# A fused linear-attention and gated feed-forward kernel: the second product from fp32r to fp16 pairs

## The chip, the cores and the metric

The kernel runs on one core of one Trainium2 chip. The metric is the device time of one execution in microseconds (us); less is better. Engines are named as in the profile: PE is TensorE's matmul, PEld its weight load, DVE is VectorE, ACT is ScalarE, POOL is GpSimd and SP is SyncE, which here issues the transfers (DMAs).

## The reference

Two stages follow each other. The first is a linear attention with the delta rule, token by token, for 4 sequences of 768 tokens and 8 heads of width 48. The second is a gated feed-forward product without an activation function.

```python
for t in range(S):
    kt, vt, bt = (k_n[:, :, t], v[:, :, t], beta[:, :, t, None])
    y[:, :, t] = np.einsum('bhd,bhde->bhe', q[:, :, t], state)
    v_old = np.einsum('bhde,bhd->bhe', state, kt)
    state = state + bt[:, :, :, None] * np.einsum('bhd,bhe->bhde', kt, vt - v_old)
...
a = x @ w_a
b = x @ w_b
return (a * b @ w_out).astype(np.float32)
```

`k_n` is k over its norm, x holds the 3072 tokens' y with 384 columns, w_a and w_b are 384 x 1536, w_out is 1536 x 384, all in fp32. So there are a *first product* (x with w_a and with w_b), a *gate* (a times b), and a *second product* (the gate's result with w_out).

## The kernel before

**Attention.** The 768 steps are cut into 24 chunks (`NCH`) of 32 tokens; one chunk holds 4 sequences x 32 tokens = 128 rows. Six groups of four chunks are prepared together: `prep` computes the norms of k and the 32 x 32 inner products, `solve` inverts the triangular systems on DVE (31 steps of two operations, or two halves of 15 for the first two groups), and `steps` runs the recurrence chunk by chunk: the state `S_ps` is copied to `sh`, multiplied with k and q (`yp`), the difference `f` is formed on DVE, multiplied by the inverse (`up`, copied to `u`), and `u` updates `S_ps` and completes `yp`. Then y is scaled and moved to `y32` (an ACT copy of one half, a DVE operation that adds the other), transposed in 32 x 32 blocks on DVE (`yT`), and split into a high and a low fp16 part (`xv`, in tiles `xb` or `late`). The tokens of two chunks make a *pair* of 256 tokens; there are twelve pairs.

**Scales.** In `prep`, the squares of v and of q are summed on ACT for a whole group (`sc`), summed over the partitions with a matmul with `ones`, and turned into one power of two per group: `z` scales y, and `fac` undoes it on the output.

**Weights.** They arrive as 12 blocks (`NFC`) of 128 of the 1536 inner columns. `weights(p)` unpacks a block on DVE (three operations of 1152 columns), takes the norm of its part of w_a and w_b (one ACT square of 768 columns with a sum, a matmul with `ones`, the rows `sw`), and scales and splits it: `wh` holds w_a and w_b as a high and a low fp16 part, `wo` holds w_out as a high and a low **fp32r** part. The low parts of the first four blocks (`LOWS`) are formed on PE: an fp32 product of a scaled unit matrix (`zi`) with the block, minus the high part by way of a product with -1 (`neg1`, `negr`), copied out by ACT. The other eight are formed on DVE.

**Feed-forward.** `moe(s, fcs)` runs over the blocks in `fcs` for the pair s. Per block: 18 matmuls of 256 columns (3 pieces of x x 3 combinations of high and low, for a and for b) into one PSUM bank; ACT copies a out (`a`); DVE multiplies b by it (`g`); ACT casts the high part and DVE subtracts the low part (`ghl`, **fp32r**, 128 x 256). `moe_out`, two blocks later (`LAG = 2`), runs 6 matmuls of 384 columns: for each of the two chunks, high x high, high x low and low x high of `ghl` (stationary) and `wo` (moving), accumulated in PSUM over the blocks of the call. At the end of a call the sum is scaled by `fac` and written or added to an accumulator, and stored at the end. The first two pairs are run in shares (`QUEUE`): blocks 0 to 5, 6 to 8 and 9 to 11, for both pairs in turn; the other ten pairs run all twelve blocks at once. In all that is 144 blocks.

**Order.** Every operation is recorded by `Plan` with a price, then put into an order by a list scheduler (`pack`) with priorities from a backward pass and from `BOOST`, `URGENCY`, and a list of random seeds (`SEEDS`), each of which shifts some priorities. `PACE` sets the earliest time of the later chunks. All engines work through their queues in that order. Since one line records everything (L515), the profile's groups are told apart by tiles, not by lines. `L506` are matmuls that only keep PE busy at the start.

**Loads.** `load` issues the transfers from SP; one-element copies on POOL (`G.tensor_copy` of a corner) hold a transfer back until an earlier one has landed.

Of the kernel before, what the change touches and what calls it, by code (L numbers as in the profile page):

```python
# [13 lines left out]
F32 = mybir.dt.float32  # L14
# [12 lines left out]
NCH = S // C  # L27
# [8 lines left out]
PARTS = [[i] for i in range(12)]  # L36
BOOST = {"first": 9e4, "prep0": 9e4, "solve0": 9e4, "steps0": 9e4, "w0": 7e4, "w1": 7e4, "w2": 6e4, "w3": 6e4, "w4": 6e4, "w5": 6e4, "prep1": 4e4, "solve1": 4e4, "steps1": 4e4, "moe": 1e5, "prep2": 0, "solve2": 0, "prep3": 0, "solve3": 0, "prep4": 0, "solve4": 0, "prep5": 0, "solve5": 0}
LOWS = 4
# [8 lines left out]
QUEUE = [(0, [0, 1, 2, 3, 4, 5]), (1, [0, 1, 2, 3, 4, 5]), (0, [6, 7, 8]), (1, [6, 7, 8]), (0, [9, 10, 11]), (1, [9, 10, 11])]  # L47
LAG = 2
PACE = (190e3, 23e3)
# [33 lines left out]
class Plan:  # L83
# [378 lines left out]
    PASS = 1  # L462
    SEEDS = (100008, 100012, 100025, 100028, 100036, 100060, 100080, 100120, 100128, 100156, 100186, 100218, 100234, 100242, 100544, 101409, 101448, 101457, 101467, 101488, 101638, 101762, 101769, 101798, 101976, 101998, 102133, 102140, 102164, 102398, 102610, 103130, 103197, 103230, 103254, 103258, 103359, 103652)
# [55 lines left out]
def tile_kernel(ctx, tc, kqt, kn, vn, begin, w, out):  # L519
# [36 lines left out]
    ghr = ring(cst, "ghl", LAG + 1, [P, 2, 256], F32R)  # L556
# [6 lines left out]
    wo = one("wo", [P, NFC, 2, DM], F32R)  # L563
# [9 lines left out]
    kb = one("kb", [P, NG * 32 + 32 + P + 2 + 6 * 384])  # L573
    bt = kb[:, 0 : NG * 32]
    mk = kb[:, NG * 32 : NG * 32 + 32 + P + 2]
    knb = kb[:, NG * 32 + 32 + P + 2 :].rearrange("p (c d) -> p c d", d=384)
# [28 lines left out]
    parity = mk[:, 32 + P :]  # L605
# [7 lines left out]
    negr = one("negr", [P, P], F32R)  # L613
# [18 lines left out]
    def weights(p):  # L632
        part = PARTS[p]
        sw = one(f"sw{p}", [P, 8])
        src = []
        for i, b in enumerate(part):
            load(b, "w")
            st, d = slots[b].rearrange("p (a l) -> p l a", l=2), spots[b]
            lo, hi = st[:, 0], st[:, 1]
            V.tensor_scalar(d, hi, 5, 2, op0=ALU.logical_shift_left, op1=ALU.logical_shift_right)  # L640
            V.scalar_tensor_tensor(d, hi, -0x40000000, d, op0=ALU.bitwise_and, op1=ALU.bitwise_or)
            V.scalar_tensor_tensor(d, lo, 29, d, op0=ALU.logical_shift_right, op1=ALU.bitwise_or)
            v = d.bitcast(F32)
            src.append(v)
            A.activation(sqh[:, 0 : 6 * P], v[:, 0 : 6 * P], AF.Square, accum_out=sw[:, i : i + 1])
            yield
        t = att()
        with plan.group():
            for i in range(len(part)):
                T.matmul(t[:, 0:1], ones, sw[:, i : i + 1], start=(i == 0), stop=(i == len(part) - 1))  # L650
        ew, zw, eo = sw[:, 4:5], sw[:, 5:6], sw[:, 6:7]
        root(ew, t[:, 0:1])
        V.tensor_scalar(zw.bitcast(I32), ew.bitcast(I32), -1.0, float((254 + 14) << 23), op0=ALU.mult, op1=ALU.add)
        V.tensor_scalar(eo, ew, ew, 2.0**-28, op0=ALU.mult, op1=ALU.mult)
        for b, v in zip(part, src):
            whole.add(b)
            h, o = halves(b)
            A.activation(h[:, 0], v[:, 0 : 6 * P], AF.Copy, scale=zw)
            A.activation(o[:, 0], v[:, 6 * P :], AF.Copy, scale=eo)
            if b < LOWS:  # L660
                V.tensor_scalar_mul(zit, eye, zw)
                for k in range(2):
                    r = slice(k * DM, k * DM + DM)
                    t = att()[:, 0:DM]
                    T.matmul(t, zit, v[:, r], start=True, stop=False)
                    T.matmul(t, neg1, h[:, 0, r], start=False, stop=True)
                    A.copy(h[:, 1, r], t)
                V.tensor_scalar_mul(zit, eye, eo)
                t = att()[:, 0:DM]
                T.matmul(t, zit, v[:, 6 * P :], start=True, stop=False)  # L670
                T.matmul(t, negr, o[:, 0], start=False, stop=True)
                A.copy(o[:, 1], t)
            else:
                V.scalar_tensor_tensor(h[:, 1], v[:, 0 : 6 * P], zw, h[:, 0], op0=ALU.mult, op1=ALU.subtract)
                V.scalar_tensor_tensor(
                    o[:, 1], v[:, 6 * P :], eo, o[:, 0].bitcast(F32), op0=ALU.mult, op1=ALU.subtract
                )
            yield
# [5 lines left out]
    facs = [None] * NCH  # L684
    xsub = [None] * (NCH // 2)
    ready = []
    ats, tts, kks, nms, gnats, zs, vsum = {}, {}, {}, {}, {}, {}, []
# [5 lines left out]
    scr = ring(cst, "sc", 3, [P, 16], F32)  # L693
# [57 lines left out]
    def prep(g):  # L751
# [65 lines left out]
        sc = scr()  # L817
        V.memset(sc[:, 0:4], 0.0)
        for i, c in enumerate(chs[::2]):
            load(c, "v")  # L820
            A.activation(
                sqh[:, 0:768], vnp(c).rearrange("p c d -> p (c d)"), AF.Square, accum_out=sc[:, 2 + i : 3 + i]
            )
            for o in range(2):
                r = slice(64 * o, 64 * o + D)
                A.activation(
                    sqh[r].rearrange("p (c a t) -> p c a t", c=2, t=32),
                    rawp(c)[r].rearrange("p c (a s t) -> p c a s t", s=2, t=32)[:, :, :, 1 - o],
                    AF.Square,
                    accum_out=sc[r, i : i + 1],  # L830
                )
        if g:
            V.tensor_add(sc[:, 2:3], sc[:, 2:3], vsum[-1])
        plan.behind = set() if g else set(ready)
        V.tensor_add(sc[:, 2:3], sc[:, 2:3], sc[:, 3:4])
        plan.behind = set() if g else set(ready)
        V.tensor_add(sc[:, 0:1], sc[:, 0:1], sc[:, 1:2])
        vsum.append(sc[:, 2:3])
        t = att()
        with plan.group():  # L840
            T.matmul(t[:, 0:1], ones, sc[:, 0:1], start=True, stop=True, skip_group_check=True)
            T.matmul(t[:, 1:2], ones, sc[:, 2:3], start=True, stop=True, skip_group_check=True)
        e, m, z, fac, zeo = sc[:, 4:6], sc[:, 6:7], sc[:, 7:8], sc[:, 8:9], sc[:, 9:11]
        root(e, t[:, 0:2])
        V.tensor_mul(m, e[:, 0:1], e[:, 1:2])
        V.tensor_scalar_max(m, m, 2.0**-100)
        V.tensor_scalar(z.bitcast(I32), m.bitcast(I32), -1.0, float((254 + 13) << 23), op0=ALU.mult, op1=ALU.add)
        V.tensor_scalar(fac, m, m, 2.0**-26, op0=ALU.mult, op1=ALU.mult)
        V.tensor_scalar_mul(zeo, parity, z)
        zs[g] = z, zeo  # L850
        for ci, c in enumerate(chs):
            facs[c] = fac
# [84 lines left out]
    def steps(g):  # L937

        chs = GROUPS[g]
        for ci, c in enumerate(chs):  # L940
# [89 lines left out]

    def moe(s, fcs):
        xt = xsub[s]
        for fc in fcs:
# [15 lines left out]
            A.copy(asb, ab[:, 0, :])  # L1049
# [4 lines left out]
            V.tensor_sub(ghl[:, 1], g32, ghl[:, 0].bitcast(F32))  # L1054
            closed.append(len(plan.ops) - 1)
            pend.append((s, fc, ghl, fc == fcs[0], fc == fcs[-1]))
# [6 lines left out]
    def moe_out(s, fc, ghl, first, last):  # L1063
        if first:
            ops[s] = [opr()[:, 0:DM] for i in range(2)]
        for i in range(2):
# [9 lines left out]
            if last:  # L1076
                c = 2 * s + i
                part = acc[c] if s < 2 else None
                final = fc == NFC - 1
                ob = obs[c % 2] if final else part  # L1080
                if part is not None and c in started:
                    V.scalar_tensor_tensor(ob, ops[s][i], facs[c], part, op0=ALU.mult, op1=ALU.add)
                else:
                    A.activation(ob, ops[s][i], AF.Copy, scale=facs[c])
                    started.add(c)
                if final:
                    SP.dma_start(out[c], ob)
# [12 lines left out]
    def run_all(gen):  # L1100
        for _ in gen:
            pass
# [29 lines left out]
    ws = [lab(f"w{i}", weights(i)) for i in range(len(PARTS))]  # L1132
# [12 lines left out]
    V.tensor_scalar_mul(negr, eye, -1.0)  # L1145
# [19 lines left out]
    run_all(ws[6])  # L1165
    merge((chain(ws[7:]), 10), (moes, 6))
# [19 lines left out]
def _layout(inputs):  # L1186
# [65 lines left out]
```

## Time and profile before

| | |
|---|---|
| median of 3 runs | 636.06 us (635.79 to 636.36) |
| the profiled execution | 635.39 us |
| its span, first to last instruction | 633.6 us |
| mean granted TensorE clock | 0.991 |
| PE / PEld / DVE / ACT / POOL busy | 615.6 / 527.5 / 405.0 / 269.0 / 47.7 us |
| first matmul of the feed-forward part | 61.73 us |
| last matmul's end, end of the span | 630.07, 633.6 us |

In the rows of groups that follow, a row reads: line, engine, operation, written tile <- read tiles, shapes, count | busy time in total, mean duration in ns | idle time of the engine just before, and what ended it. In the timeline a row is a run of like instructions: its start, its length, the engine and the operation, with the count last. The lengths of matmuls overlap, so what a run takes of PE is the next run's start minus its own. The waits list who waited for whom: total us, times, longest. An fp32 matmul is two instructions in the trace, an fp32r or 16-bit one is one; fp32r is written f32.

### The profile page before, as it was taken

How to read it: one execution, taken by the hardware profiler on the slowest of the kernel's cores; microseconds unless marked ns; L12 is line 12 of the kernel's file. 1: busy time of each engine (PE TensorE's matmuls, PEld its weight loads, DVE VectorE, ACT ScalarE, POOL GpSimd, SP SyncE). 2: the span in 40 equal slices, each digit the busy share in tenths (PEclk: the TensorE clock that was granted, in tenths of full speed). 3: DMA queues.
4: the chain of work that ended last, by engine and by line, in shares of the span. 5: the costliest groups of instructions: out<-in, count | busy, mean ns of one | idle time of the engine just before them, and what ended most of it. 6: DMA issues, size and time to landing. Idle time of an engine off the chain costs nothing.

```text
span 633.6 us, 26978 instructions
## 1 busy us (share of the span) xinstructions
PE 615.6 (97%) x12204; PEld 527.5 (83%) x12204; DVE 405.0 (64%) x1059; ACT 269.0 (42%) x599; POOL 47.7 (8%) x134
## 2 busy tenths in 40 slices
PE   6989999999999999999999999999999999999997
PEld 5756888888888888888888888888888888888886
DVE  5886899879664887378863488733438854332232
ACT  2455872556436238332382233733232253332222
POOL 0111210110012002000020000200000000000000
PEclk9969999999999999999999999999999999999999
DMA  8655540441265200025000051000000000000000
GB/s 316 177 148 156 161 115 22 128 141 50 86 199 146 81 26 4 21 71 160 18 28 20 25 157 66 2 27 2 4 28 2 1 27 5 3 26 1 26 1 25
DMA packets 20754, 42.80 MB, mean 68 GB/s; under 512 B 2208, under 2 KB 5280, under 8 KB 20640
## 3 DMA queue, kind: packets, MB, share of 16 engines
q1 hardware_dynamic: 20640, 41.08, 21.0%
q8 instruction: 95, 1.56, 1.1%
q14 instruction: 19, 0.16, 0.1%
HBM read 36.36 MB, written 4.72 MB: 65 GB/s over the span
## 4 chain that ended last, share of the span: by engine, by line
PE 77%; DVE 5%; ACT 4%; issue 1%; ACTq 0%
PE bank L515 74%; PE S_ps L515 3%; DVE b L515 2%; ACT sqf L515 1%; DVE tmp L515 1%; ACT tt L515 1%; DVE g L515 1%; ACT ghl L515 1%; DVE ghl L515 1%; ACT a L515 0%; DVE at L515 0%; DVE s L515 0%; DVE f L515 0%; DVE ss L515 0%; DVE sc L515 0%
## 5 line engine op out<-in xcount | busy, mean ns | idle before, releaser
L515 PEld LDWEIGHTS <-wh 128*128 128x128 f16 x2592 | 242.7, 98 | 48.0 <-issue 19.5
L515 PE MATMUL bank<-xb,wh 128*128 128x256 f16 x2160 | 257.3, 273 | 0.7 <-DVE g L515 0.6
L515 PE MATMUL bank<-wo,ghl 128*128 128x384 f32 x864 | 187.7, 352 | 1.2 <-issue 1.1
L515 PEld LDWEIGHTS bank<-wo,ghl 128*128 128x128 f32 x864 | 144.0, 188 | 6.4 <-issue 1.9
L515 ACT COPY a<-bank 128x256 f32<-128x256 f32 x144 | 53.3, 371 | 200.0 <-PE bank L515 199.8
L515 DVE TENSOR_TENSOR g<-bank,a 128x256 f32<-128x256 f32 x144 | 60.7, 422 | 115.2 <-ACT a L515 113.8
L515 DVE TENSOR_TENSOR ghl<-g,ghl 128x256 fp32r<-128x256 f32 x144 | 61.1, 424 | 39.3 <-ACT ghl L515 37.2
L515 ACT CAST ghl<-g 128x256 fp32r<-128x256 f32 x144 | 58.2, 404 | 61.2 <-DVE g L515 53.3
L515 PE MATMUL bank<-late,wh 128*128 128x256 f16 x432 | 52.7, 273 | 0.3 <-issue 0.3
L515 DVE TENSOR_TENSOR b<-b,tmp 128x31 f32<-128x31 f32 (+20 forms) x154 | 49.9, 324 | 3.6
L515 DVE TENSOR_TENSOR tmp<-b,b 128x31 f32<-128x31 f32 (+20 forms) x154 | 49.5, 322 | 3.5
L515 PE MATMUL bank<-rawb 48*32 48x64 f32 x1280 | 21.2, 217 | 5.2 <-DMA rawb<-in_kqt 3.6
L515 PEld LDWEIGHTS bank<-rawb 48*32 48x32 f32 x1280 | 18.7, 107 | 8.8 <-issue 4.8
L515 DVE SCALAR_TENSOR_TENSOR y<-bank,sc,y 128x384 f32<-128x384 f32 x23 | 14.2, 617 | 17.8 <-ACT y L515 17.3
L515 ACT COPY sh<-S_ps 112x768 f32<-112x768 f32 x23 | 18.2, 793 | 16.7 <-PE S_ps L515 16.7
L515 PEld LDWEIGHTS bank<-sh,rawb 48*64 48x64 f32 x1216 | 19.6, 134 | 5.1 <-issue 3.6
L515 DVE TENSOR_TENSOR f<-vnb,bank 128x384 f32<-128x384 f32 x38 | 19.7, 545 | 5.8 <-PE bank L515 5.8
L515 PEld LDWEIGHTS bank<-f,tt 32*32 32x32 f32 x1472 | 17.5, 105 | 6.0 <-issue 4.4
L515 PE MATMUL bank<-sh,rawb 48*64 48x48 f32 x1216 | 22.1, 220 | 0.3 <-issue 0.3
L515 POOL COPY late<-late 1x1 int32<-1x1 int32 x44 | 13.1, 302 | 118.9 <-DMA late<-in_w 49.1
L515 ACT ACTIVATE sqf<-rawb 48x1024 bf16<-48x1024 f32 x20 | 21.1, 1056 | 0.4
L515 PE MATMUL bank<-u,at 32*32 32x48 f32 x1536 | 21.2, 202 | 0.0
(123 smaller groups left out, 562.9 us busy)
## 6 DMA issues: line engine op xcount, KB each, us to landing
late<-in_w SPq DMA_DIRECT2D x40, 288.0 KB, 3.2
rawb<-in_kqt SPq DMA_DIRECT2D x32, 256.0 KB, 2.8
out<-late SPq DMA_DIRECT2D x24, 192.0 KB, 1.9
vnb<-in_vn SPq DMA_DIRECT2D x10, 384.0 KB, 3.7
kb<-in_kn SPq DMA_DIRECT2D x9, 384.0 KB, 3.7
wh<-in_w SPq DMA_DIRECT2D x8, 288.0 KB, 3.0
rawb<-in_kqt SPq DMA_DIRECT2D x2, 1024.0 KB, 7.1
late<-in_kqt SPq DMA_DIRECT2D x8, 256.0 KB, 2.8
```

Source lines behind the costliest of these rows:

```text
L515: fn(*(self.place(a, lease) for a in args), **{k: self.place(a, lease) for k, a in kw.items()})
```

## The change

1. `wo` and `ghl` become fp16, so the second product's 864 matmuls run on pairs of fp16 numbers, as the first product's do. `negr` goes; `neg1` serves both.
2. fp16 has a narrow range, so the scales are finer. Each **token** gets a power of two from its own sum of squares of y: after `y32`, four ACT squares of 96 columns with sums (`ysum`), one bf16 matmul of 4 columns with a 0/1.03 mask (`near`) that adds the sums over the four rows of a token, three DVE operations of 4 columns that make the power of two `z`, and one DVE product of 384 columns that scales `y32` in place. The factor to undo it (`facs[c]`) is made by a POOL product with a mask (`own4`), a DVE reduce over 4 columns and one more DVE operation. The group's sums over v and q (`sc`) and their scales go.
3. Each weight **block** gets norms of w_a, w_b and w_out apart: three ACT squares of 384 columns, one matmul of 3 columns, and some more small DVE operations, among them a bound and a factor per block.
4. Each **share** of blocks gets a common factor (`common`): the largest bound over its blocks. The ACT copy of `a` carries the block's factor relative to it, and the output's factor is multiplied by it (`fac`, once per chunk and call).
5. The shares of the first two pairs are four of three blocks (0 to 2, 3 to 5, 6 to 8, 9 to 11); before there were three of 6, 3 and 3.
6. `LOWS` goes from 4 to 6, `PACE` from (190e3, 23e3) to (185e3, 22e3), `PASS` from 1 to 4, and the seeds are others, so the whole order is another.

```diff
-LOWS = 4
+LOWS = 6
...
-    ghr = ring(cst, "ghl", LAG + 1, [P, 2, 256], F32R)
+    ghr = ring(cst, "ghl", LAG + 1, [P, 2, 256], F16)
...
-    wo = one("wo", [P, NFC, 2, DM], F32R)
+    wo = one("wo", [P, NFC, 2, DM], F16)
...
+    def common(lo, hi):
+        top = one(f"top{lo}_{hi}", [P, 2])
+        part = one(f"part{lo}_{hi}", [P, hi - lo])
+        V.tensor_reduce(top[:, 0:1], bounds[:, lo:hi], AX.X, ALU.max)
+        V.tensor_scalar_max(top[:, 0:1], top[:, 0:1], 2.0**-100)
+        V.tensor_scalar(
+            top[:, 1:2].bitcast(I32), top[:, 0:1].bitcast(I32), -1.0, float((254 - 42) << 23), op0=ALU.mult, op1=ALU.add
+        )
+        V.tensor_scalar(part, factors[:, lo:hi], top[:, 1:2], None, op0=ALU.mult)
+        scales[lo, hi] = top, part
...
-            A.activation(sqh[:, 0 : 6 * P], v[:, 0 : 6 * P], AF.Square, accum_out=sw[:, i : i + 1])
...
+        for i, o in enumerate((2 * DM, 0, DM)):
+            A.activation(sqh[:, 0:DM], v[:, o : o + DM], AF.Square, accum_out=sw[:, i : i + 1])
...
+        T.matmul(t[:, 0:3], ones, sw[:, 0:3], start=True, stop=True)
+        root(sw[:, 3:6], t[:, 0:3])
...
-                A.activation(y32, yp[0][:, 0:384], AF.Copy, scale=zeo[:, 1:2])
-                V.scalar_tensor_tensor(y32, yp[1][:, 0:384], zeo[:, 0:1], y32, op0=ALU.mult, op1=ALU.add)
+                A.activation(y32, yp[0][:, 0:384], AF.Copy, scale=parity[:, 1:2])
+                V.scalar_tensor_tensor(y32, yp[1][:, 0:384], parity[:, 0:1], y32, op0=ALU.mult, op1=ALU.add)
+            y4 = y32.rearrange("p (b d) -> p b d", b=4)
+            ys, z = ssr(), zr()
+            for b in range(4):
+                A.activation(ysr(), y4[:, b], AF.Square, accum_out=ys[:, b : b + 1])
+            t = att()
+            T.matmul(t[:, 0:4], near, ys.bitcast(BF16).rearrange("p (b l) -> p l b", l=2)[:, 1], start=True, stop=True)
+            zi = z[:, 0:4].bitcast(I32)
+            V.tensor_scalar(zi, t[:, 0:4].bitcast(I32), 1, 0x3FC00000, op0=ALU.logical_shift_right, op1=ALU.bitwise_and)
+            V.tensor_scalar(zi, zi, -1.0, float(408 << 22), op0=ALU.mult, op1=ALU.add)
+            V.tensor_scalar(zi, zi, 0x7F800000, None, op0=ALU.bitwise_and)
+            V.tensor_mul(y4, y4, z[:, 0:4].unsqueeze(2).broadcast_to([P, 4, 96]))
+            G.tensor_mul(z[:, 4:8], z[:, 0:4], own4)
+            V.tensor_reduce(facs[c], z[:, 4:8], AX.X, ALU.add)
+            V.tensor_scalar(
+                facs[c].bitcast(I32), facs[c].bitcast(I32), -1.0, float(254 << 23), op0=ALU.mult, op1=ALU.add
+            )
...
-            A.copy(asb, ab[:, 0, :])
+            lo_, hi_ = share(fc, len(fcs))
+            A.activation(asb, ab[:, 0, :], AF.Copy, scale=scales[lo_, hi_][1][:, fc - lo_ : fc - lo_ + 1])
...
-            V.tensor_sub(ghl[:, 1], g32, ghl[:, 0].bitcast(F32))
+            V.tensor_sub(ghl[:, 1], g32, ghl[:, 0])
...
+                fac = facr()
+                V.tensor_scalar(fac, facs[c], top, facs[c], op0=ALU.mult, op1=ALU.mult)
```

Three places of the order show what moves. The first is DVE at the second chunk's y (`y_96`), whose x the first block of the feed-forward part waits for. Before:

```order
101 L515 SCALAR_TENSOR_TENSOR y_96<-bank_62,sc_127,y_96 128x384
102 L515 STREAM_TRANSPOSE yt_97<-y_96 128x384
103 L515 TENSOR_SCALAR zi<-kb,sw_137 128x128
104 L515 TENSOR_TENSOR xb<-yt_97,xb 128x4x3x32
105 L515 TENSOR_TENSOR f_72<-vnb,bank_65 128x384
```

Now, some twenty rows further on (the row that adds the two halves of `y_96` stands four rows ahead of this piece):

```order
122 L515 TENSOR_SCALAR z_137<-bank_66 128x4
123 L515 TENSOR_SCALAR z_137<-z_137 128x4 x2
124 L515 TENSOR_TENSOR y_96<-y_96,z_137 128x384
125 L515 STREAM_TRANSPOSE yt_97<-y_96 128x384
126 L515 TENSOR_SCALAR zi<-kb,sw_172 128x128
127 L515 TENSOR_SCALAR sw_173<-bank_64 128x3
128 L515 TENSOR_REDUCE fac_139<-z_137 128x1
129 L515 TENSOR_SCALAR sw_173<-sw_173 128x3
130 L515 TENSOR_SCALAR fac_139<-fac_139 128x1
131 L515 TENSOR_SCALAR sw_173<-sw_173 128x3
132 L515 TENSOR_TENSOR xb<-yt_97,xb 128x4x3x32
```

Four operations stand ahead of the transpose, and two for the factor (`fac_139`) between it and x's low part; the reduce takes what POOL wrote to `z_137`. The second place is PE ahead of its first product of x with the weights (`xb,wh`; `f` and `u` are a chunk's, `sw` a weight block's norms, `zi` and `neg` make a block's low part). Before:

```order
175 L515 MATMUL bank_64<-b_3_71,tt_88 32x16 x32
176 L515 MATMUL bank_62<-sw_138,ones 128x1
177 L515 MATMUL bank_63<-late,zi 128x384
178 L515 MATMUL bank_64<-b_3_71,kb 128x256
179 L515 MATMUL bank_63<-wo,negr 128x384
180 L515 LDWEIGHTS wh
181 L515 MATMUL bank_62<-xb,wh 128x256
```

Now:

```order
257 L515 MATMUL bank_62<-u_74,at_79 32x48
258 L515 MATMUL bank_63<-u_74,at_79 32x48
259 L515 MATMUL bank_61<-wh,zi 128x384
260 L515 LDWEIGHTS neg_114
261 L515 MATMUL bank_61<-wo,neg_114 128x384
262 L515 LDWEIGHTS wh
263 L515 MATMUL bank_66<-xb,wh 128x256
```

Before, two chunks' updates and three blocks' low parts stood ahead of the first product; now the third chunk's update (`u_74,at_79` is its last matmul) and a fourth block's low part do too. The third place is POOL, where a chunk's product with `own4` (`z_136`) stands among the copies that hold transfers back. Before:

```order
18 L515 COPY late<-rawb 1x1
19 L515 COPY late<-vnb 1x1
20 L515 COPY late<-late 1x1 x6
21 L515 COPY wh<-late 1x1 x2
22 L515 COPY wh<-wh 1x1 x2
```

Now:

```order
18 L515 COPY late<-rawb 1x1
19 L515 COPY late<-vnb 1x1
20 L515 COPY late<-late 1x1 x2
21 L515 ISA
22 L515 TENSOR_TENSOR z_136<-z_136,kb 128x4
23 L515 COPY late<-late 1x1 x4
24 L515 COPY wh<-late 1x1 x2
```

The product of the first chunk stands behind two of the six copies that gate the pieces of the next weight blocks, and four of them stand behind it.

More of the change, by code (lines that the diff above doesn't have):

```diff
@@ L612, in tile_kernel @@
     neg1 = one("neg1", [P, P], F16)
-    negr = one("negr", [P, P], F32R)
+    own4 = mk[:, 32 + P + 2 : 32 + P + 6]
+    near = mk[:, 32 + P + 6 :].bitcast(BF16)
     sqf = one("sqf", [P, 768])
@@ L630, in halves @@
         return wh[:, fc].bitcast(F16).rearrange("p (l a) -> p l a", l=2), wo[:, fc]
[L632 to L644, printed above, removed]
-            A.activation(sqh[:, 0 : 6 * P], v[:, 0 : 6 * P], AF.Square, accum_out=sw[:, i : i + 1])
-            yield
-        t = att()
[L648 to L668, printed above, removed]
-                t = att()[:, 0:DM]
[L670 to L678, printed above, removed]
@@ new lines, in tile_kernel @@
+    bounds, factors = one("bounds", [P, NFC]), one("factors", [P, NFC])
+    scales = {}
+    def common(lo, hi):
[8 more added lines that the diff above has]
+        scales[lo, hi] = top, part
@@ L692, in tile_kernel @@
     nmr = ring(cst, "nm", 3, [P, 32], F32)
-    scr = ring(cst, "sc", 3, [P, 16], F32)
+    ysr = ring(cst, "ys", 2, [P, 96], BF16)
+    ssr = ring(cst, "ysum", 2, [P, 4], F32)
+    facr = ring(cst, "fac", 4, [P, 1], F32)
+    zr = ring(cst, "z", 2, [P, 8], F32)
+    facs = [one(f"fac{c}", [P, 1]) for c in range(NCH)]
     tmpt = one("tmp", [P, 256])
@@ L816, in prep @@
             rest[0]()
-        sc = scr()
-        V.memset(sc[:, 0:4], 0.0)
-        for i, c in enumerate(chs[::2]):
+        for c in chs[::2]:
             load(c, "v")
[L821 to L850, printed above, removed]
         for ci, c in enumerate(chs):
-            facs[c] = fac
             plan.behind = set() if g else set(ready)
@@ L1029, in mm, with share @@
         T.matmul(*a, **k)
+    def share(fc, n):
+        return next((lo, hi) for lo, hi in SHARES if lo <= fc < hi and hi - lo == n)
     def moe(s, fcs):
@@ L1061, in tile_kernel, with moe_out @@
     ops = {}
-    def moe_out(s, fc, ghl, first, last):
+    def moe_out(s, fc, ghl, first, last, top):
         if first:
@@ L1081, in moe_out @@
                 if part is not None and c in started:
-                    V.scalar_tensor_tensor(ob, ops[s][i], facs[c], part, op0=ALU.mult, op1=ALU.add)
+                    V.scalar_tensor_tensor(ob, ops[s][i], fac, part, op0=ALU.mult, op1=ALU.add)
                 else:
-                    A.activation(ob, ops[s][i], AF.Copy, scale=facs[c])
+                    A.activation(ob, ops[s][i], AF.Copy, scale=fac)
                     started.add(c)
@@ L1130, in tile_kernel @@
     moes = lab("moe", moe_stream())
-    ws = [lab(f"w{i}", weights(i)) for i in range(len(PARTS))]
+    ws = [lab(f"w{i}", weights(i)) for i in range(NFC)]
     pr = [lab(f"prep{g}", prep(g)) for g in range(NG)]
@@ L1144, in tile_kernel @@
     V.tensor_scalar_mul(neg1, eye, -1.0)
-    V.tensor_scalar_mul(negr, eye, -1.0)
     for _ in range(6):
```

78 lines of the change are left out of this document (60 added, 18 removed).

## The prediction

> **What bounds the kernel now.** I read the page first: the span, the busy shares, and the chain that ended last.
>
> ```profile
> span 633.6 us, 26978 instructions
> ...
> PE 615.6 (97%) x12204; PEld 527.5 (83%) x12204; DVE 405.0 (64%) x1059; ACT 269.0 (42%) x599; POOL 47.7 (8%) x134
> ...
> PE 77%; DVE 5%; ACT 4%; issue 1%; ACTq 0%
> ```
>
> PE is busy nearly throughout and carries 77% of the chain. A busy PE is not proof of a PE bound, since matmuls overlap, so I next read busy time by stage, with cuts at the first block of the feed-forward part (about 62 us) and at the end of weight unpacking (about 163 us).
>
> ```profile
> core 0: us, PE busy (x) PEld busy (x) DVE busy (x) ACT busy (x) POOL busy (x), PEclk, DMA share, GB/s
> 30.00:64.00 34.00, 30.13 (x982) 21.30 (x973) 27.24 (x63) 17.71 (x39) 6.35 (x17) 0.85 0.55 155
> 64.00:160.00 96.00, 95.54 (x2600) 80.33 (x2588) 84.77 (x210) 57.29 (x125) 11.54 (x32) 1.00 0.35 104
> 160.00:630.00 470.00, 467.14 (x8256) 406.84 (x8252) 272.25 (x728) 182.20 (x414) 26.57 (x67) 1.00 0.14 42
> ```
>
> There are two regimes. From 160 us on, PE is full (467 of 470) and DVE has 42% to spare: there the time is the sum of matmul spacings. Between 64 and 160 us PE is full too (95.5 of 96), but DVE is at 88% behind it. So a change that takes work from PE pays fully late, and one that gives work to DVE can cost early. The granted clock is 1.00 in both, so it plays no part in the sum.
>
> What a matmul costs PE is its spacing, not its duration. The timeline of PE, late in the run with nothing but feed-forward blocks, gives spacings as differences of starts:
>
> ```profile
> start us, us, engine line op out<-in xcount [idle before <-releaser]
> 572.05 0.78 PE L515 MATMUL bank<-wo,ghl 128*128 128x384 f32 x3
> 572.67 1.16 PE L515 MATMUL bank<-xb,wh 128*128 128x256 f16 x9
> 573.58 1.81 PE L515 MATMUL bank<-wo,ghl 128*128 128x384 f32 x9
> 575.24 3.12 PE L515 MATMUL bank<-xb,wh 128*128 128x256 f16 x27
> 578.12 1.30 PE L515 MATMUL bank<-wo,ghl 128*128 128x384 f32 x6
> 579.26 2.14 PE L515 MATMUL bank<-xb,wh 128*128 128x256 f16 x18
> 581.16 1.30 PE L515 MATMUL bank<-wo,ghl 128*128 128x384 f32 x6
> 582.30 0.94 PE L515 MATMUL bank<-xb,wh 128*128 128x256 f16 x7
> ```
>
> Nine first-product matmuls (256 wide, fp16) take 0.91 us, 27 take 2.88: 1.97 more for 18 more, 0.109 us each. Three second-product matmuls (384 wide, fp32r, which the profile lists as f32) take 0.62, nine take 1.66: 0.173 each, plus about 0.1 that every run of them costs at its start. A whole block, 18 and 6 matmuls, takes 582.30 - 579.26 = 3.04 us, and there are 144 blocks.
>
> **The second product in fp16.** The counts stay (864 matmuls of 384 columns). Durations by type:
>
> ```profile
> L515 PEld LDWEIGHTS <-wh 128*128 128x128 f16 x2592 | 242.7, 98 | 48.0 <-issue 19.5
> L515 PE MATMUL bank<-xb,wh 128*128 128x256 f16 x2160 | 257.3, 273 | 0.7 <-DVE g L515 0.6
> ...
> L515 PEld LDWEIGHTS bank<-wo,ghl 128*128 128x128 f32 x864 | 144.0, 188 | 6.4 <-issue 1.9
> ...
> L515 PE MATMUL bank<-wh,neg 128*128 128x384 f16 x8 | 2.5, 328 | 0.0
> ```
>
> The run of `neg` shows a 384-wide fp16 matmul already: 328 ns against 273 for 256 columns, 55 ns for 128 columns more. So I expect a spacing of 109 + 55 = 164 ns in place of 173. The start of a run should cost nothing more: the fp32r weight load of 188 ns can't hide behind a 109 ns matmul, one of 98 ns does. A block becomes 18 x 0.109 + 6 x 0.164 = 2.95, a gain of 0.09 us; times 144 that is **13.0 us**. Bounds: only the slope (9 ns x 864 = 8) below; above, the 55 ns read as 53 and every run start free, 16.
>
> **Two more blocks through PE** (`LOWS` from 4 to 6). Each adds three fp32 and three fp16 matmuls of 384 columns. The timeline of PE has two such fp32 products (two passes each) and one fp16:
>
> ```profile
> 66.18 1.46 PE L515 MATMUL bank<-wh,zi 128*128 128x384 f32 x4
> 67.47 0.33 PE L515 MATMUL bank<-wh,neg 128*128 128x384 f16 x1
> 67.73 0.47 PE L515 MATMUL S_ps<-u,kb 32*48 32x48 f32 x22
> ```
>
> 1.29 / 2 = 0.65 and 0.26, so 3 x 0.91 = 2.7 per block and **+5.4 us**, fully exposed since PE is full there (bounds 4.9, if the fp16 ones take 164 ns, to 6). The four products with `negr` become fp16 as well: some hundredths, taken as nothing.
>
> **The norms on PE.** Removed: twelve fp32 sums in six groups (24 passes). Added: 24 one-pass matmuls of 4 columns, one per chunk.
>
> ```profile
> L515 PE MATMUL bank<-sc,ones 128*128 128x1 f32 x24 | 3.2, 237 | 0.0
> ```
>
> 24 passes leave, 24 come: 0 (bounds -2 to +2, if a lone pass costs 0.05 or 0.2). The weight sums go from one column to three: nothing.
>
> **The chain of y.** Each chunk's y now passes four squares on ACT, the matmul with `near`, three small DVE operations, and a scaling of 384 columns before it is transposed. This is some 3 us longer, but the state's recurrence (`sh`, `f`, `u`, `S_ps`) doesn't go through y, so it delays only when a pair's x is ready. That is on the path once, ahead of the first block. There the order has a third chunk and a fourth block of weights put ahead of the first product, work that PE did later before. I count no loss for the start (bounds 0 to 3).
>
> **DVE up to 160 us.** The durations:
>
> ```profile
> L515 DVE SCALAR_TENSOR_TENSOR wh<-wh,sw 128x768 f16<-128x768 f32 x4 | 4.1, 1016 | 0.9 <-ACT wh L515 0.9
> ...
> L515 DVE SCALAR_TENSOR_TENSOR wo<-wh,sw,wo 128x384 fp32r<-128x384 f32 x4 | 2.4, 610 | 0.0
> ...
> L515 DVE TENSOR_SCALAR sw<-sw 128x1 int32<-128x1 int32 x36 | 5.2, 147 | 0.5
> ...
> L515 DVE TENSOR_TENSOR vnb<-vnb,nm 128x384 f32<-128x384 f32 x8 | 4.3, 549 | 0.0
> ...
> L515 DVE SCALAR_TENSOR_TENSOR acc<-bank,sc,acc 128x384 f32<-128x384 f32 x4 | 2.3, 607 | 0.0
> ```
>
> Added: for eight chunks five small operations at 0.147 and one of 384 columns at 0.549, 8 x 1.3 = 10.3 (the reduce over four columns isn't in the trace; it lies between a small one and these 0.55, and I take 0.15). For twelve blocks two more small ones each, and four per share, 44 x 0.147 = 6.5. The fourth share costs four more accumulations at 0.607 and 16 products for the factors, 4.8. Removed: the low halves of two blocks, 2 x (1.016 + 0.610) = 3.3, and some eleven small ones in each of two groups, 3.3. Net +15.0 us. DVE's idle time in 64 to 160 us is 96 - 84.8 = 11.2 us, and PE itself takes about 3.6 us longer there (5.4 for the two blocks, less 20 blocks x 0.09). If all of that idle can be filled, 0.2 us is left over; if none, 11.4. What DVE waited for decides:
>
> ```profile
> engine line waited for: us in total, times, longest us
> DVE g L515 <- ACT a L515: 6.2, 8, 2.0
> DVE y L515 <- ACT y L515: 2.4, 1, 2.4
> DVE ghl L515 <- ACT ghl L515: 2.2, 6, 0.5
> ```
>
> (DVE's waits from 60 to 180 us.) These 10.8 us are waits for PE's own results by way of ACT; a DVE that is behind doesn't wait for them. So I take a value nearer the low end: PE loses **3.5 us** to a late `g` or `ghl`. After 160 us DVE's 42% absorb the other 16 chunks (16 x 1.3 = 21 of 198 us idle) at no cost; without that cover they would cost up to 21. On ACT, `a` gains a scale by a column (about 0.1 us x 144), four squares per chunk come, and the squares of v and q go; ACT is busy 57 of 96 us early and 182 of 470 later: nothing.
>
> **The end.** The last matmuls, the scaled copy and the store stay: nothing. The factor of a chunk and share is one small product, made long before.
>
> **The sum** against the profiled execution's 635.39 us (span 633.6): 635.4 - 13.0 + 5.4 + 3.5 = 631.3. The median of the runs is 0.7 above the profiled one, so I forecast **632.0** (own range 628.5 to 634.7).
>
> **Rivals.**
>
> *The cover holds.* All DVE work fits into its idle time, and the stall is 0: 628.5; with the upper bound for the product 625.5. For it: the 10.8 us of waits above. Against: DVE at 88% already. Chance 0.22.
>
> *DVE takes over ahead of 160 us (the other side).* `g` and `ghl` come late because the scaling of y stands in the same queue. Behind it the reduce of `fac` waits for a product on POOL, whose queue is full of one-element copies that wait for transfers:
>
> ```profile
> POOL late L515 <- DMA late<-in_w: 49.1, 27, 3.3
> ```
>
> A copy there waits 1.8 us on average. While the reduce waits, the transpose of y, `g` and `ghl` behind it on DVE wait too, and PE for them. Stall 11.4: 628.5 + 11.4 = 639.9. It decides from a stall of 6.3 us (no gain to be measured) and 8.8 us (slower). For it: no DVE slack in the order, and a queue in place of a DVE-only path. Against: the POOL product follows its DVE source by a full 384-column scaling. Chance 0.22, half of it within 0.2% of no change.
>
> *The product doesn't get faster.* If the 173 ns are the price of 384 columns as such and not of the type, only the run starts gain (about 3 us): 632.0 + 10 = 642. Against: 109 ns for 256 columns, 2 over what 55 ns per 128 give. Chance 0.08.
>
> *384 columns overlap more.* If fp16 matmuls of any width followed each other at 109 ns, 864 x 0.064 = 55 us would go: 577. Against: the 55 ns between the two widths' durations. Chance 0.02. The Trainium skill, "TensorE: Matmul & The Clock Gate", section "Back-to-back issue gap", states a sustained 81 ns for 128 columns and 131 for 512 in streams of weight load and matmul, by which I estimate 114 ns for 384. By that rule 256 columns would take 98 ns, and the trace has 109, so it doesn't hold here.
>
> **How the numbers follow.** Forecast 0.46, the cover holds 0.22, DVE 0.22, not faster 0.08, overlap 0.02, rest nil. Over 0.2% (1.3 us, about what can be told from no change here) faster: 0.46 + 0.22 + 0.02 = 0.70. Within it: 0.11 + 0.03 = 0.14. Slower: 0.11 + 0.05 = 0.16. The range 625.5 to 639.5 leaves out half of the last three cases' upper ends and the overlap, under 0.2.
>
> **What would show it.** In the profile after: `wo,ghl` as f16 in runs that grow by 0.164 us per matmul; a late block of 18 and 6 in 2.95 us; six `neg` rows for `wo`; DVE above 95% from 70 to 160 us, and PE waiting for DVE there by some 3 us. Wrong if a late block takes 3.0 or more; if PE has no idle early (the cover holds); or if PE's idle ahead of 160 us grows by over 8 us, or waits for POOL appear on DVE.

## The result, and the profile after

The changed kernel takes 631.2 us (median of 4 runs, 629.4 to 632.5) against 636.0 before; the ratio is 0.992, 95% interval [0.990, 0.995]. The forecast was 632.0. Two later repeats of it gave 632.9 and 633.0 (10 and 11 runs, 629.8 to 638.5), so the gain is 3 to 5 us. The profiled execution took 632.46, the longest of its four, at the lowest mean granted clock of them (0.978; the kernel before had 0.991 in its profile).

The head of the page after, to be read against that of before:

```profile
span 630.7 us, 27334 instructions
...
PE 611.6 (97%) x12218; PEld 477.6 (76%) x12218; DVE 435.4 (69%) x1215; ACT 286.0 (45%) x773; POOL 56.4 (9%) x158
...
PEclk7869899999999999999999999998999999999999
...
PE 75%; DVE 13%; ACT 4%; DMA 3%; issue 3%; SPq 0%; POOL 0%; DVEq 0%; ACTq 0%; POOLq 0%
```

DVE has 30 us more work and PE 4 us less. In the chain, DVE has grown from 5% to 13% and `issue` from 1% to 3%, and a wait for weights at the start (`DMA late<-in_w`, 3%) is new. `issue` is idle time for which the profile shows no cause. The clock row begins 78698 where it began 99699. The stages (columns as in the table by stage of the prediction):

```profile
0.00:30.00 30.00, 26.37 (x324) 21.73 (x324) 20.48 (x57) 4.89 (x9) 3.20 (x18) 0.83 0.75 249
30.00:64.00 34.00, 31.22 (x1075) 20.63 (x1075) 28.34 (x72) 24.58 (x74) 7.43 (x17) 0.85 0.49 146
64.00:160.00 96.00, 94.45 (x2463) 72.13 (x2462) 89.28 (x247) 61.03 (x171) 11.26 (x38) 0.98 0.34 103
160.00:630.00 470.00, 459.58 (x8359) 363.12 (x8358) 297.30 (x843) 195.54 (x521) 34.53 (x85) 1.00 0.14 44
```

Between 64 and 160 us DVE went from 84.8 to 89.3 of 96 us, which is 93% and not over 95%, and PE's granted clock is 0.98. What PE waited for in this stretch:

```profile
PE bank L515 <- DVE f L515: 0.6, 2, 0.4
PE bank L515 <- issue: 0.5, 1, 0.5
PE bank L515 <- ACT ys L515: 0.3, 1, 0.3
PE bank L515 <- ACT sqf L515: 0.3, 1, 0.3
```

Waits for `g` and `ghl`, of which the prediction expected 3.5 us, are not among them. After 160 us PE was busy 467.1 of 470 us before, now 459.6. A part of that is only that its last matmul ends earlier (at 627.2 us, not 630.1); PE's waits from 160 us on went from 2.7 to 7.3 us. The late timeline shows what a block costs now (start, length, ..., count):

```profile
571.17 1.15 PE L515 MATMUL bank<-xb,wh 128*128 128x256 f16 x9
572.15 1.14 PE L515 MATMUL bank<-wo,ghl 128*128 128x384 f16 x6
573.13 2.13 PE L515 MATMUL bank<-xb,wh 128*128 128x256 f16 x18
575.10 0.65 PE L515 MATMUL bank<-wo,ghl 128*128 128x384 f16 x3
575.58 4.09 PE L515 MATMUL bank<-xb,wh 128*128 128x256 f16 x36
...
581.96 3.09 PE L515 MATMUL bank<-wo,ghl 128*128 128x384 f16 x18
584.88 1.36 PE L515 MATMUL bank<-xb,wh 128*128 128x256 f16 x11
...
```

Six second-product matmuls take 573.13 - 572.15 = 0.98 us and eighteen 584.88 - 581.96 = 2.92: 0.162 each, with nothing left for the start of a run. Eighteen first-product ones take 1.97. A block is 2.95 us, as forecast.

### The profile page after: what moved, and what is told of

It is laid out like the page before. It is cut to its first block, busy times and chain, and to the rows that moved or that the text cites. A ratio compares the mean times of both kernels' runs of the same rounds, so it can differ in the third digit from the quotient of the medians.

```text
span 630.7 us, 27334 instructions
## 1 busy us (share of the span) xinstructions
PE 611.6 (97%) x12218; PEld 477.6 (76%) x12218; DVE 435.4 (69%) x1215; ACT 286.0 (45%) x773; POOL 56.4 (9%) x158
## 3 DMA queue, kind: packets, MB, share of 16 engines
q8 instruction: 95, 1.56, 1.0%
## 4 chain that ended last, share of the span: by engine, by line
PE 75%; DVE 13%; ACT 4%; DMA 3%; issue 3%; SPq 0%; POOL 0%; DVEq 0%; ACTq 0%; POOLq 0%
PE bank L515 73%; DMA late<-in_w 3%; DVE b L515 3%; PE S_ps L515 3%; DVE tmp L515 2%; DVE wh L515 2%; DVE late L515 1%; DVE ghl L515 1%; DVE g L515 1%; ACT sqf L515 1%; ACT ys L515 1%; ACT ghl L515 1%; DVE f L515 0%; ACT wh L515 0%; SPq L515 0%
## 5 line engine op out<-in xcount | busy, mean ns | idle before, releaser
L515 PEld LDWEIGHTS <-wh 128*128 128x128 f16 x2592 | 250.8, 98 | 49.0 <-issue 6.2
L515 PE MATMUL bank<-wo,ghl 128*128 128x384 f16 x864 | 166.2, 327 | 1.3 <-DVE g L515 0.7
L515 ACT ACTIVATE a<-bank,part 128x256 f32<-128x256 f32 x144 | 68.0, 473 | 155.7 <-PE bank L515 152.3
L515 PEld LDWEIGHTS <-ghl 128*128 128x128 f16 x864 | 80.3, 98 | 44.5 <-issue 2.1
L515 DVE TENSOR_TENSOR ghl<-g,ghl 128x256 f16<-128x256 f32 x144 | 61.4, 429 | 35.6 <-ACT ghl L515 33.4
L515 ACT CAST ghl<-g 128x256 f16<-128x256 f32 x144 | 57.9, 404 | 59.2 <-DVE g L515 47.2
L515 DVE SCALAR_TENSOR_TENSOR y<-bank,kb,y 128x384 f32<-128x384 f32 x23 | 14.2, 617 | 28.4 <-ACT y L515 28.3
L515 ACT ACTIVATE ys<-y 128x96 bf16<-128x96 f32 x96 | 26.0, 273 | 6.6 <-DVE y L515 6.4
L515 POOL TENSOR_TENSOR z<-z,kb 128x4 f32<-128x4 f32 x24 | 9.8, 409 | 201.8 <-DVE z L515 193.3
L515 PEld LDWEIGHTS bank<-u,at 32*32 32x32 f32 x1536 | 19.1, 108 | 4.8 <-issue 4.0
```

Source lines behind the costliest of these rows:

```text
L515: fn(*(self.place(a, lease) for a in args), **{k: self.place(a, lease) for k, a in kw.items()})
```

## Experiments

All variants keep the changed kernel's order on every engine; operations are replaced, added or left out where they are issued, and the pieces of code below are shortened and written as if the source itself had been changed. "Repeated" is the changed kernel run beside them. Intervals for one variant against another are worked out from the two ratios to the kernel before, as the root of the sum of their squared half-widths.

**The changed kernel, repeated.**

> The changed kernel once more, unaltered, as the yardstick for the variants. The changed kernel had 631.2 us as its median, with 3 us between its runs, where the kernel before had 0.6. If its losses come from a fixed order, this run shows the same ones at the same places: half clock from 9 to 18 us, half clock near 68 us, an issue gap of 1.7 us near 431 us. If they depend on when the hardware's clock window falls, some of them are at other places or gone, and the time lies between 629 and 633 us.

Measured: 632.9 us (0.994 of before [0.991, 0.997]). Half clock came early again (0.77 up to 30 us), and nearly all the gaps of PE that the profile calls issue stood at the same instructions. From 200 to 560 us:

```profile
PE bank L522 <- issue: 3.7, 5, 1.2
PE S_ps L522 <- issue: 1.6, 1, 1.6
PE bank L522 <- ACT tt L522: 1.0, 1, 1.0
PE bank L522 <- DVE g L522: 0.7, 1, 0.7
...
```

So most of PE's late idle time is of one kind, and it repeats.

**The second product back in fp32r.**

```diff
-    ghr = ring(cst, "ghl", LAG + 1, [P, 2, 256], F16)
+    ghr = ring(cst, "ghl", LAG + 1, [P, 2, 256], F32R)
...
-    wo = one("wo", [P, NFC, 2, DM], F16)
+    wo = one("wo", [P, NFC, 2, DM], F32R)
...
+    negr = one("negr", [P, P], F32R)
...
-            T.matmul(t, neg1, o[:, 0], start=False, stop=True)
+            T.matmul(t, negr, o[:, 0], start=False, stop=True)
```

> The changed kernel in its own order, with the second product's operands (g and wo, high and low parts) back in fp32r; one of six small products per early block goes with them. Theory (the fp16 matmuls themselves bring the gain, 0.09 us a block x 144): 13.0 us slower than the changed kernel, some 644, a late block of 18 and 6 at 3.04 us and runs of the second product growing by 0.173 us per matmul. Rival 1 (the new order or the new shares bring the gain, not the type): within 3 us of the changed kernel. Rival 2 (only the start of a run was saved): late blocks of 3.0, 6 to 8 us slower.

Measured: 646.8 us, 13.9 above the repeated kernel (12 to 18 by the intervals). Its late timeline:

```profile
588.42 1.29 PE L520 MATMUL bank<-wo,ghl 128*128 128x384 f32 x6
589.55 2.14 PE L520 MATMUL bank<-xb,wh 128*128 128x256 f16 x18
591.45 0.78 PE L520 MATMUL bank<-wo,ghl 128*128 128x384 f32 x3
...
595.92 1.81 PE L520 MATMUL bank<-wo,ghl 128*128 128x384 f32 x9
597.58 1.16 PE L520 MATMUL bank<-xb,wh 128*128 128x256 f16 x9
598.49 3.37 PE L520 MATMUL bank<-wo,ghl 128*128 128x384 f32 x18
601.70 3.12 PE L520 MATMUL bank<-xb,wh 128*128 128x256 f16 x27
```

Eighteen take 3.21 and nine 1.66, so 0.172 per matmul and 0.1 per run; a block of 18 and 6 takes 3.03. Eighteen first-product matmuls take 591.45 - 589.55 = 1.90 here and 1.97 between fp16 ones, so of the 0.1 only some 0.03 is lost. Of the 0.09 us a block, some 0.06 comes from the spacing and the rest from the edges of the runs. The type brings the gain, and all of it: both rivals fall.

**Low parts of blocks 4 and 5 on DVE.**

```diff
-                T.matmul(t, zit, v[:, r], start=True, stop=False)
-                T.matmul(t, neg1, h[:, 0, r], start=False, stop=True)
-                A.copy(h[:, 1, r], t)
...
+            V.scalar_tensor_tensor(h[:, 1], v[:, 0 : 6 * P], zw, h[:, 0], op0=ALU.mult, op1=ALU.subtract)
+            V.scalar_tensor_tensor(o[:, 1], v[:, 6 * P :], zo, o[:, 0], op0=ALU.mult, op1=ALU.subtract)
```

> The low parts of blocks 4 and 5 come from DVE again (one operation of 768 and one of 384 columns per block, 1.016 + 0.610 us), not from PE, everything else in the changed kernel's order. Theory (PE is the bound ahead of 160 us and DVE's idle time takes more): the 5.1 us of PE work that the trace shows for the two blocks come back, 3 to 5 us faster than the changed kernel, 626 to 628. Rival (DVE is the bound there by now): 3.3 us more on DVE in a stretch where it is busy 93%, so PE waits for g or ghl instead, and the time is the same or up to 2 us longer.

Measured: 630.7 us, 2.2 less than repeated (-0.6% to +0.1%), which lies between the two. The profile says something else than either. Start against start of the same operations, it is 4.4 us *later* than the repeated kernel at 133 us, with PE's work gone but new waits from 60 to 105 us (the first five of the list):

```profile
PE bank L522 <- DVE y L522: 2.6, 1, 2.6
PE S_ps L522 <- ACT u L522: 1.1, 1, 1.1
PE S_ps L522 <- issue: 1.0, 1, 1.0
PE bank L522 <- ACT sqf L522: 0.7, 1, 0.7
PE bank L522 <- DVE g L522: 0.7, 1, 0.7
...
```

It catches up between 280 and 470 us, where nothing was changed but the place of PE's code: issue gaps of 0.9 us from 200 to 560 us, against 5.3. Beside the variant below that has its code in the same place and all of PE's work (36 instructions fewer, 626.9 us) it is 3.8 us *slower* (1 to 6 by the intervals; 4.1 start against start at the end). So the 3.3 us on DVE cost more there than the 5 us on PE, and moving these low parts to PE was no loss.

**The chain of y left out in chunks 0 to 7, with and without its matmuls.**

```diff
-            for b in range(4):
-                A.activation(ysr(), y4[:, b], AF.Square, accum_out=ys[:, b : b + 1])
...
-            V.tensor_mul(y4, y4, z[:, 0:4].unsqueeze(2).broadcast_to([P, 4, 96]))
-            G.tensor_mul(z[:, 4:8], z[:, 0:4], own4)
-            V.tensor_reduce(facs[c], z[:, 4:8], AX.X, ALU.add)
+            G.memset(facs[c], 1.0)
```

> For the chunks 0 to 7 the scaling by token norms is left out (four squares on ACT, the matmul with near, the operations on z, the scaling of y, the reduce for fac; the factors are set to one), in the changed kernel's order; the other 16 chunks keep it. About 10 us of DVE work go from the stretch up to 160 us, and 0.5 us of PE. Theory (the cover held, DVE cost PE next to nothing): 0 to 1.5 us faster than the changed kernel. Rival (the prediction's term, PE loses 3.5 us to a late g or ghl): 4 us faster. Second rival (the chain of y delays the first feed-forward block): faster by 1 to 2 us, all of it ahead of 75 us.

> For the chunks 0 to 7 the scaling by token norms is left out on ACT, DVE and POOL (squares, the operations on z, the scaling of y, the reduce for fac; factors and sums are set to one), but PE keeps every instruction, the matmul with near too, so that its code is the same, instruction by instruction, as in the changed kernel. The run that left out the matmuls as well was 6.3 us faster by the medians, of which its profile shows 3.1 us between 420 and 470 us, where it leaves nothing out: there the issue gaps of PE (1.63 and 1.25 us) were gone. Theory (DVE's work on y costs next to nothing, the gain was the shifted code): 0 to 2 us faster than the changed kernel repeated, 631 to 633, with the issue gaps near 431 and 470 us back. Rival (the prediction's term, DVE's work costs PE 3.5 us or more ahead of 160 us): 628.5 or less, and the gain lies ahead of 180 us.

Measured: 626.6 us without the eight small matmuls, 630.6 with them (0.986 [0.983, 0.988] and 0.992 [0.989, 0.995] of before). The difference, 4 us (1 to 7 by the intervals), is for eight matmuls of 0.17 us that others mostly hide, and for their place in PE's code. The variant that kept them has the gap in `S_ps` back, in the repeated kernel's place. What DVE's and ACT's work on y costs is 632.9 - 630.6 = 2.3 by medians (not told apart from 0), and start against start 0.6 to 1.1 us from 73 to 340 us, all of it gained ahead of the first feed-forward blocks. Why DVE's 10 us cost so little stands in DVE's own waits from 64 to 160 us without them, where the changed kernel's list has no wait for `a` at all:

```profile
DVE g L522 <- ACT a L522: 3.0, 2, 1.8
DVE sw L522 <- PE bank L522: 1.3, 2, 0.9
...
```

Less work on DVE there mostly becomes waiting for PE's results. The cover of the prediction is elastic.

**More work on DVE.**

```diff
-            V.transpose(yT, y32)
+            for _ in range(3 if c < 8 else 1):
+                V.transpose(yT, y32)
```

> For the chunks 0 to 7 the transpose of y runs three times in place of once (0.57 us each): 9.1 us more on DVE, nearly what the scaling by token norms put there. Theory (DVE has some idle time left ahead of 160 us, but not this much: 6.7 us idle of 96 in the changed kernel): 2 to 6 us slower than the changed kernel repeated, with PE waiting for g, ghl or y there. Rival 1 (the waits of DVE are elastic and still take it up): within 1 us. Rival 2 (DVE is the bound already): 9 us slower.

Measured: 637.7 us, 4.8 above repeated (3 to 7); the profiled execution is its longest, 642.0. Start against start it loses 3 us up to 137 us and 5 to 6 up to 180, and 4 more between 290 and 375 us, mostly in issue gaps:

```profile
299.73 0.70 PE L522 MATMUL bank<-xb,wh 128*128 128x256 f16 x5 [2.04 <-issue]
348.93 1.05 PE L522 MATMUL bank<-late,wh 128*128 128x256 f16 x8 [1.12 <-issue]
```

So about half of DVE's next 9 us would be paid for, though not all of it by waits for DVE: from 60 to 182 us PE's issue gaps grew from 0.5 to 1.7 us, while its waits for DVE's `f`, `xb` and `fac` sum to 1.1, against 0.6 for `f` alone. By this the change has used up most of the cover.

**Where the code lies.** Four large idle matmuls near 20 us make room for 64 tiny ones (112 instructions more), or 9 or 4 of them are made twice as wide in place of as many others (36 or 16 fewer):

```diff
-        self.nc.tensor.matmul(self.pool[-1][0:128, 0:256], one, one.unsqueeze(1).broadcast_to([P, 2, 128]), ...)
+        m = 2 if j < 9 else 1
+        self.nc.tensor.matmul(self.pool[-1][0:128, 0:256 * m], one, one.unsqueeze(1).broadcast_to([P, 2 * m, 128]), ...)
```

> 64 tiny idle matmuls in place of four large ones in the idle time near 20 us, nothing else: PE's code shifts by somewhat over a hundred instructions, the work and its order stay. Theory (the gaps on PE that the profile puts down to issue are waits for the next piece of code, at fixed places of the instruction stream): the gaps at 427, 431 and 470 us lie at other instructions, about 56 of the small matmuls earlier in the code, and their sum changes by a microsecond or two either way. Rival (they belong to the instruction at which they stand): the gap in the run of S_ps near 431 us stays between its 61st and 62nd matmul.

> The changed kernel once more, as the yardstick on the same chip for the three runs beside it. By the runs so far 631 to 633 us, with the same issue gaps on PE as before: 0.6 to 1.2 us near 288 and 292 us, 1.6 to 1.7 near 431.

> Nine of the 26 idle matmuls near 20 us are twice as wide and nine others go, so PE has 36 instructions less and the same idle work; all else is the changed kernel. From there on PE's code lies as in the variant with the low parts of blocks 4 and 5 on DVE, whose profile shows 0.9 us of issue gaps from 200 to 560 us where the changed kernel has 4.6 to 5.3. Theory (the gaps are waits for code at every 256th instruction of PE, and what they cost depends on which products lie there): the gaps at 288 to 293, 431 and 470 us go or shrink as in that variant, 2 to 4 us faster than the changed kernel repeated, about 629. Rival (the gain of that variant after 420 us came from its lateness, not from its code): no change.

> As the run beside it with four idle matmuls twice as wide and four gone: 16 instructions less on PE, as in the variant without the whole chain of y in chunks 0 to 7 (626.6 us), of which 4 us stood between it and the one that kept PE's instructions. Theory (code): 1.5 to 3 us faster than the changed kernel repeated, gaps from 200 to 560 us of some 2.0 us in sum. Rival (that variant's gain was DVE's and ACT's work on y together with PE's): no change.

Measured: 633.9 us with 112 more, 633.0 repeated, **626.9** with 36 fewer (0.986 [0.983, 0.989] of before; 0.991 [0.987, 0.995] of the repeated kernel), 629.4 with 16 fewer (0.990 [0.987, 0.993]). The same place of PE's timeline, first repeated:

```profile
426.95 1.10 PE L522 MATMUL bank<-rawb 48*32 48x64 f32 x64 [0.65 <-issue]
427.97 0.92 PE L522 MATMUL S_ps<-u,kb 32*48 32x48 f32 x61
430.53 0.29 PE L522 MATMUL S_ps<-u,kb 32*48 32x48 f32 x3 [1.63 <-issue]
430.75 1.64 PE L522 MATMUL bank<-wo,ghl 128*128 128x384 f16 x9
```

With 36 instructions fewer:

```profile
426.07 1.10 PE L525 MATMUL bank<-rawb 48*32 48x64 f32 x64 [0.65 <-issue]
427.10 0.93 PE L525 MATMUL S_ps<-u,kb 32*48 32x48 f32 x64
427.96 1.64 PE L525 MATMUL bank<-wo,ghl 128*128 128x384 f16 x9
```

The gap in the midst of 64 like matmuls, which wait for nothing, is gone. Start against start, this variant is 0.5 to 0.9 us later than the repeated kernel from 67 to 280 us and 4.7 us earlier from 471 us on, and it gains at these gaps. Its median granted clock is 0.980 (the repeated kernel's is 0.984), so the clock doesn't bring the gain. With 16 fewer the gap stands further on, among the `wo,ghl`, and is smaller:

```profile
429.35 0.82 PE L525 MATMUL bank<-wo,ghl 128*128 128x384 f16 x4 [0.66 <-issue]
```

PE's 12,218 matmuls and as many weight loads are 24,436 instructions, and the queue that brings code moved 95 pieces:

```profile
q8 instruction: 95, 1.56, 1.0%
```

That is 64 bytes each and 257 per piece; the variant with 112 more has 96 pieces. The trace also has when each piece came. In the repeated kernel a transfer of this queue starts at 427.99 and one at 468.01 us, 2.5 us ahead of the end of the gaps near 431 and 470. In all thirteen profiles of the changed order, every issue gap but the one near 427 us ends 2.2 to 3.1 us after the start of such a transfer. Late in the run, where only feed-forward blocks are left, the transfers come some 15 us apart.

Counted in PE's order (matmuls and weight loads), the repeated kernel's gaps near 288 and 292 us stand at the 12,700th and 12,956th instruction, 256 apart; the shifted ones have theirs at the 12,956th too, with 112 more in the midst of `rawb` (293.55 us), with 36 fewer in the midst of `sh,rawb` (292.85 us). The gaps near 431 and 470 us, at 17,812 and 20,110, are 19 and 28 times 256 on from there, less 8 and 14. So these gaps belong to the count, not to the operation. What one costs depends on what lies ahead of it: 64 fp32 matmuls of 32 or 48 columns take 128 instructions in 0.9 us, eighteen of the feed-forward part 36 in 1.97. The places are fixed, but what they cost is not: in the profile of the second repeat (629.8 us) the gaps near 288 and 292 us are absent, against what was expected of it, and that near 431 is 1.4 us. The 0.65 us ahead of `rawb` near 427 us are another matter. This gap stands ahead of the same matmul in every variant, against what the first theory expected; the last transfer of code starts 9 to 12 us ahead of its end in all of them but the one with 112 more; and its cause is open.

**Two more idle matmuls at the start.**

```diff
-                    for _ in range(n):
+                    for _ in range(n + 2 * (n == 7)):
```

> Two more idle matmuls (nine, not seven) ahead of the first Gram products, nothing else: PE's gap of 1.9 us ahead of them shrinks by about 1.6 us. Theory (this gap is what takes the clock down from 9 to 18 us): the granted clock of the first 30 us rises from 0.77-0.83 to over 0.95, the first product with b comes 1.5 us earlier, and the time is 1 to 1.5 us shorter than the changed kernel repeated. Rival (the half clock comes from the gaps after the first Gram products, or falls where the hardware's window falls): the clock stays below 0.9 and the time within 1 us.

Measured: 634.6 us (0.998 [0.995, 1.000]), nothing gained. The first Gram matmuls ran at full clock (128 in 1.99 us, where the changed kernel took 3.17), but the clock was 0.89 up to 30 us and 0.80 from 30 to 64 us, and the eight instructions moved the code to a worse place: 9.7 us of issue gaps in the whole profile, 6.8 repeated. The half clock stays open: up to 30 us the mean granted clock was 0.77 to 0.94 in every profile of the changed order, at differing places, and its share in the time wasn't separated. An estimate: the median granted clock is 0.987 in the 60 runs of the kernel before that stand beside these variants and 0.983 in 25 of the changed one, and among the runs of each, 0.01 less clock goes with 3 to 4 us more, so some 1 to 2 us. That is a correlation only (-0.6 and -0.55).

**Low parts of blocks 4 and 5 left out.**

```diff
-        if b < LOWS:
+        if b in (4, 5):
+            G.memset(h[:, 1], 0.0)
+            G.memset(o[:, 1], 0.0)
+        elif b < LOWS:
```

> The low parts of blocks 4 and 5 are left out altogether (zeros), so neither PE, ACT nor DVE makes them; PE's code is 36 instructions shorter from about 65 us on. Theory: the 5.1 us of PE work go and 2 to 4 us of issue gaps too, so 7 to 9 us faster than the changed kernel repeated, and 5 us faster than the run that only shifts the code by 36 instructions. Rival (ahead of 100 us the first chunks' chain sets the time, and PE's work on the two blocks is partly hidden): 2 to 3 us faster than that run only.

Measured: 627.0 us, 6 less than repeated, but just what the shift of the code by 36 brings (626.9): the 5 us of PE work are worth 0.0, give or take 2.8; start against start the variant is 1.3 us ahead at 100 us and 0.7 at the end. PE's waits from 64 to 100 us without them:

```profile
PE bank L522 <- DVE y L522: 2.0, 1, 2.0
PE S_ps L522 <- ACT u L522: 1.6, 1, 1.6
PE bank L522 <- DVE f L522: 0.6, 2, 0.4
...
```

And with them, code in the same place:

```profile
PE bank L525 <- ACT sqf L525: 0.7, 1, 0.7
PE bank L525 <- ACT ys L525: 0.2, 1, 0.2
PE bank L525 <- DVE f L525: 0.2, 1, 0.2
```

The work on PE stood in front of waits for the first chunks' chain on DVE and ACT (`y`, `u`, `f`). Without it PE waits for those: the rival holds, more strongly than it was put.

## Why the prediction came out right

*The second product, -13.0.* Right in mechanism and size: 0.162 per matmul (164 ns was taken), no cost at a run's start, 2.95 us a block, 13.9 us when undone. The rivals "doesn't get faster" and "overlaps more" fall. Three of their numbers were off, without touching the forecast: 109 ns is 1 under 2 x 55, not 2 over; the run starts alone would have gained 5 us, not 3 (0.09 less 6 x 0.009, times 144); and 577 takes off the step from 173 to 164 ns twice (632.0 less 864 x 0.055 is 584). The Trainium skill, "TensorE: Matmul & The Clock Gate", section "Back-to-back issue gap", would have 384 columns at an estimated 114 ns; the trace has 162.

*Two more blocks through PE, +5.4, "fully exposed since PE is full there".* This is the step that failed. The matmuls take the time that was counted, but leaving them out gains nothing that can be told from 0 beyond what the code's place gives (1 us by the traces), since DVE's `y` and ACT's `u` end the wait instead. A PE that is busy 95.5 of 96 us before, and 94.5 after, isn't proof that its work sets the end there: the list scheduler puts work that can be done at any time into the waits of a serial chain, and the share of busy time shows it as full.

*DVE up to 160 us, +3.5, "PE loses 3.5 us to a late `g` or `ghl`".* This path wasn't there: from 64 to 160 us PE waits for neither, and its waits sum to 1.7 us. Taking the work on y out of eight chunks brings 1.0 us by the traces and 2.3 by the medians (not told apart from 0), and by the traces it is gained ahead of the first feed-forward blocks, where the prediction counted nothing for the chain of y (bounds 0 to 3). So the rival "the cover holds" is nearer the truth in this stretch. That DVE's waits for PE's results by way of ACT are elastic was the reason given for a small term, and the run with less on DVE shows it. The rival "DVE takes over" begins just past the present load (9 us more cost 4.8, and the low parts on DVE, 3.3 us, cost 3.8 with the code in the same place); its wait for POOL (`fac` behind `z`) is 0.3 us in the profile.

*The norms on PE, 0.* From each start to the next and without gaps, the 24 `ysum` matmuls take 1.2 us and the 24 `sc` passes took 2.4: within the bounds.

*The start, 0.* Not shown to be right: PE's first product with `b` comes 1.5 us later than before (30.82 us, not 29.32), and the first feed-forward block at 70.6 us, not 61.7. Half clock in the first Gram matmuls isn't what delays `b`: with 16 instructions fewer and with two more idle matmuls the first 128 of them ran in 1.99 us, as before, and `b` still came at 30.82 and 30.77. How much of the later first block is made up by the work put ahead of it wasn't tried.

*What the sum left out* is the place of PE's code. The profile before had 5.5 us of issue gaps (2.1 after 60 us), the profile after 6.5 (5.1), and the new order could be had for 6.1 us less by taking 36 idle instructions away. That nothing was counted for it, for the clock or for the start was balanced by the low parts and by DVE, which were counted at 5.4 and 3.5. So the number was right partly by luck, because errors cancel: 13.9 us of gain from the product, against 3 to 5 measured, leaves 9 to 11 us of loss. Of these, PE's waits after 160 us show 4.6 in the first profile (7.3 less 2.7; 2.8 of it is issue gaps, which went from 1.8 to 4.6), and the chain of y 1 to 2. The rest, at the start and in the order ahead of 160 us, is not resolved; the clock may have a part in it.

## What to carry to other kernels

Price a change of type by the spacing in long runs of the trace: that number was right to 2%. Where PE is full, ask whether what fills it could have waited; take a piece of it out, and compare with a variant whose code lies in the same place, before calling it the bound. And when a kernel issues long rows of tiny matmuls, look for idle time put down to `issue` inside a row of like instructions: some instructions more or less ahead of it can be worth 1%, at no cost in work, so two versions of a kernel should not be compared by one placement of their code.

## What the runs showed of the hardware

- PE's code arrives in pieces of 256 instructions while the kernel runs (95 pieces, 1.56 MB), and at a piece's edge, behind rows of 64 tiny fp32 matmuls above all, PE can stop for 0.2 to 2.0 us. The gap ends 2.2 to 3.1 us after the start of a transfer of code. All issue gaps of a profile, with the one of 0.65 us that is of another kind, sum to 3.8 to 11.4 us; the variants with the least (3.8 with 36 instructions fewer, 3.8 without the chain of y) are the two fastest.
- An fp16 matmul of 384 columns follows another after 0.162 us and one of 256 columns after 0.109; in fp32r 384 columns take 0.172 and a run's start 0.1 more, of which the run behind it gives some 0.07 back (1.90 us for eighteen, not 1.97).
- The granted clock was 0.50 from 9 to 18 us in the first profile of the changed kernel, where the kernel before had 1.00 with a longer gap ahead of the same matmuls (2.8 us, not 1.9), and 0.58 from 432 to 434 us, behind an issue gap of 1.7 us; behind one of 1.63 us in the repeated kernel it stayed at 1.00, and behind one of 1.63 in the variant that kept the y matmuls it was 0.50 from 431 to 433 us. The Trainium skill, "TensorE: Matmul & The Clock Gate", section "What's actually happening", has a window of 3.4 us that is free-running and doesn't start with the kernel; that like gaps bring the clock down in one execution and not in another agrees with it.
